# Order of the first batches' loads, v products and transposes, and place of the output transposes, in an attention and MLP kernel on one core

## The chip, the core and the metric

The kernel runs on one core of a Trainium2 chip. A core has five engines that run their own instruction streams in order and wait for one another through semaphores: TensorE (PE in the profile, its weight loads PEld), VectorE (DVE), ScalarE (ACT), GpSimd (POOL) and SyncE (SP, which only issues DMAs here). The metric is the device time of one execution in microseconds; the time before is the median of five runs.

## The reference

Two stages in a row, in float32, with 8 batches, 8 heads, 576 positions and head size 64:

```python
scores = scale * np.matmul(q, k.transpose(0, 1, 3, 2))
log_f = np.log(np.clip(f, 0.0001, 1.0))
cum = np.cumsum(log_f, axis=-1)
decay = cum[:, :, :, None] - cum[:, :, None, :]
causal = np.triu(np.ones((S, S), dtype=bool), k=1)
scores = np.where(causal, -1000000000.0, scores + decay)
attn = softmax(scores)            # exp(scores - max), divided by its row sum
x = (attn @ v) with heads side by side: 4608 tokens x 512
h = x @ w_in                      # 512 x 2048
g = h * (1.0 / (1.0 + np.exp(-h)))
out = g @ w_out                   # 2048 x 512
```

## The kernel before

The decay between two positions splits into a factor of the row, which the softmax's division cancels, and a factor of the column, exp(-cum + half), which is multiplied into v. So v with an extra column of ones times these weights gives numerator and denominator of the softmax in one product, and no maximum is taken.

**Heads of the sequences.** The first 128 positions of each batch are handled first ("0" in the names: `turn0`, `scores0`, `out0`, `back0`), for all heads of a batch at once. `turn0(b, 0)` turns q and `turn0(b, 1)` turns k with 16 matmuls each; ScalarE copies the q part to `qT`, VectorE the k part to `kT`. `scores0` makes the scores (a mask is added before by `ban0` or multiplied later by `mask0`) and ScalarE takes the exponential. `convert_v0` multiplies v by the weights `w_bf` (GpSimd). `out0` multiplies the exponentials with that v, and VectorE divides. `back0` turns the result with TensorE, and a copy puts it into the input `x` of the MLP. Batches 0 to 3 are done ahead of all else; 4 to 7 in the two calls of `two_more`, between MLP pieces.

**Rest of the sequences.** The loop over `m` takes two steps `n` = 2m and 2m + 1, each a batch's pair of heads (`b, p = divmod(n, 4)`) with the positions from 128 on. `prepare(n)` issues, for pair n + 2, the casts to bf16 on GpSimd (`cast_qk`) and a DMA transpose on SP (`transposes`, tile `qkT`, three buffers), the loads of pair n + 4, and for the next batch the loads of v on SP and the v products `convert_v` on GpSimd. `scores(n, c)` does one of three parts of the scores and exponentials; `attend(n)` the products with v, and VectorE divides into `xr`. `back(m)` turns a pair's outputs into `x`: by seven TensorE transposes into the tile `tx` and two VectorE copies where `BY_DMA[m]` is false (m = 0 to 3 and 15), by two DMA transposes on SP otherwise.

**MLP.** The tokens are cut into 13 groups `g`: three of heads, one of each batch's rest, two of tails. For each group, M1 has 16 chunks (`m1_chunk`: four matmuls into `hp`, tanh on ScalarE into `th`, `(th + 1) * hp` on VectorE into `gt`), and M2 has four parts for each 128 tokens (`m2_part`: four matmuls of 512 columns into `po`; after the fourth part ScalarE copies `po` to `osb`, and a store is queued). One M1 chunk or one M2 part is a piece. The queued stores are issued on GpSimd's queue by `slot`.

**Order.** It is written out by hand: each engine runs its instructions in the order in which the program emits them. Pieces of the MLP are put between the attention's steps by `fill(us, least, ends)`: `plan` lists as many pieces as the estimated time `us` holds, `wanted` chooses between M1 and M2, and `ends = (1, 0)` asks for an M2 piece first. A group's M1 may start once the group is in `ready`. In the loop over m, `slot(us, 1, 0)` calls `fill`, then issues the stores that were queued before it, then counts down `pending`, the list of groups that become ready some slots after their `back`. All PSUM tiles of `hp`, `po`, `dn`, `tx`, `tp` share four buffers (tag "big"); `sc` has two of its own.

The weights of the MLP are loaded in quarters, converted to bf16 on the way, by DMAs on GpSimd's queue (`load_w_in(0)` to `(3)`, `load_w_out`); so are the heads' q and k and v of batches 2 to 7.

Of the kernel before, what the change touches and what calls it, by code (L numbers as in the profile page):

```python
# [18 lines left out]
def kernel(  # L19
# [10 lines left out]
    nc = tc.nc  # L30

    B, H, S, D = q.shape
# [5 lines left out]
    SM = 512  # L38
    ST = S - SM
# [148 lines left out]
    def load_w_in(i):  # L188
        c0, c1 = i * DFF // WQ, (i + 1) * DFF // WQ
        nc.gpsimd.dma_start(out=w_in_bf[:, :, c0:c1], in_=w_in_v[:, :, c0:c1])  # L190
# [29 lines left out]
    for i in range(2):  # L220
        for g in range(2):
            nc.vector.tensor_copy(
                out=sel[:, i, :].rearrange("p (u w r) -> p u w r", u=2, w=2)[:, g, :, :],
                in_=ident_bf[:, :].rearrange("p (r u i w) -> p u i w r", u=2, i=2, w=2)[
                    :, g, i, :, :
                ],
            )

    def keep_warm(n):
# [7 lines left out]
        out=f_sb[:, :], in0=f_sb[:, :], scalar1=1e-4, scalar2=1.0, op0=ALU.max, op1=ALU.min  # L237
# [3 lines left out]
    wexp = setup.tile([BH, S + ST], FP32, name="wexp")  # L241
    nc.scalar.activation(out=f_sb[:, :], in_=f_sb[:, :], func=ACT.Ln)

    def weights_scan():
        nc.vector.tensor_tensor_scan(
            out=cum[:, :],
            data0=f_sb[:, :],
            data1=f_sb[:, :],
            initial=0.0,
            op0=ALU.add,  # L250
            op1=ALU.bypass,
        )
        nc.vector.tensor_scalar_mul(out=half[:, :], in0=cum[:, S - 1 : S], scalar1=0.5)
        nc.scalar.activation(
            out=wexp[:, 0:S], in_=cum[:, :], func=ACT.Exp, bias=half[:, 0:1], scale=-1.0
        )
        nc.vector.tensor_scalar(
            out=ban[:, :, :],
            in0=tri[:, None, :].to_broadcast([P, NP, P]),
            scalar1=-1.0,  # L260
            scalar2=30000.0,
            op0=ALU.add,
            op1=ALU.mult,
        )
        nc.vector.tensor_copy(out=wexp[:, S : S + ST], in_=wexp[:, SM:S])

    def weights():
        wps = pbig.tile([P, NM + 1, BH], FP32, name="wps", tag="big")
# [9 lines left out]
    def turn0(b, i):  # L278
        src = qk0[b]
        if i == 0:  # L280
            qT0[b] = qktp.tile([P, NP, P], BF16, name="qT0", tag="qT0", bufs=2)
        dst, evac = ((qT0[b], nc.scalar.copy), (kT0[b], nc.vector.tensor_copy))[i]
        tp = pbig.tile([P, NP, NRUN, RUN], FP32, name="tp", tag="big")
        for c in range(RUN):
            for j in range(2):
                nc.tensor.matmul(  # L286
                    tp[j * D : (j + 1) * D, :, :, c].rearrange("p a r -> p (a r)"),
                    lhsT=src[:, i, c * D : (c + 1) * D],
                    rhs=sel[:, j, :],
                    start=True,  # L290
                    stop=True,
                )
        evac(
            out=dst[:, :, :].rearrange("p a t -> p (a t)"),
            in_=tp[:, :, :, :].rearrange("p a r c -> p (a r c)"),
        )

    def ban0(b):
        sc = psc.tile([P, 2, NP, P], FP32, name="sc", tag="sc")
        for i in range(2):  # L300
            nc.tensor.matmul(
                sc[:, i, :, :].rearrange("p a t -> p (a t)"),
                lhsT=ident_bf[:, :],
                rhs=ban[:, :, :].rearrange("p a t -> p (a t)"),
                start=True,
                stop=False,
            )
        return sc

    def scores0(b, sc=None):  # L310
        t = qT0.pop(b)
        fresh = sc is None
        u = upool.tile([P, 2, NP, P], BF16, name="u", tag="u")
        u0[b] = u
        if fresh:
            sc = psc.tile([P, 2, NP, P], FP32, name="sc", tag="sc")
        for p in range(NP):
            for i in range(2):
                r = slice(i * D, (i + 1) * D)
                nc.tensor.matmul(  # L320
                    sc[:, i, p, :],
                    lhsT=kT0[b][r, p, :],
                    rhs=t[r, p, :],
                    start=fresh,
                    stop=fresh or p == NP - 1,
                )
        nc.scalar.activation(
            out=u[:, :, :, :].rearrange("p i a t -> p (i a t)"),
            in_=sc[:, :, :, :].rearrange("p i a t -> p (i a t)"),
            func=ACT.Exp,  # L330
            scale=scale,
        )
# [4 lines left out]
            out=x, in0=x, in1=tri[:, None, :].to_broadcast([P, H, P]), op=ALU.mult  # L337
        )

    def convert_v0(b):  # L340
        nc.gpsimd.tensor_tensor(
            out=v0[b][:, :, :],
            in0=vf0.pop(b)[:, :, :],
            in1=w_bf[:, 0, b * H : (b + 1) * H, None].to_broadcast([P, H, D + 1]),
            op=ALU.mult,
        )
# [338 lines left out]
    def plan(us_):  # L685

        a, c, kinds = at["m1"], at["m2"], []
        while us_ > 0:
            k = wanted(a, c)
            if not k:  # L690
                break
            kinds.append(k)
            if k == 1 and M1[a][1] == 0:
                begin[M1[a][0]] = (0, c)
            us_ -= (4 * (GW[M1[a][0]] / 2.4 + 2.5) if k == 1 else 4 * (DM / 2.4 + 2.5)) / 1000
            a, c = a + (k == 1), c + (k == 2)
        return kinds

    def fill(us_, least=0, ends=(0, 0)):

        left = us_ + at["left"]
        kinds = plan(left)
        n2 = kinds.count(2)
        kinds += [0] * (least - len(kinds))
        if any(ends) and n2 and 0 not in kinds:
            e0 = 1 if ends[0] else 0
            e1 = 1 if ends[1] and n2 > e0 else 0
            n1, mid = len(kinds) - n2, []
            inner = n2 - e0 - e1
            for x in range(n1 + inner):  # L710
                mid.append(2 if (x + 1) * inner // (n1 + inner) > x * inner // (n1 + inner) else 1)
            if inner and mid[-1] == 2 and e1:
                mid = mid[::-1] if not (e0 and mid[0] == 2) else mid
            kinds = [2] * e0 + mid + [2] * e1
        for k in kinds:
            t = step(k)
            if t is None:
                at["left"] = 0.0
                return
            left -= t / 1000  # L720
        at["left"] = left
# [5 lines left out]
    turn0(0, 0)  # L727
    keep_warm(1)
    turn0(0, 1)
    bans = [ban0(0), ban0(1)]  # L730
    scores0(0, bans[0])
    weights()
    setup_pool.__exit__(None, None, None)
    gpool = ctx.enter_context(tc.tile_pool(name="gpool", bufs=2))
    convert_v0(0)
    load_w_in(0)
    turn0(1, 0)
    turn0(1, 1)
    turn0(2, 0)
    turn0(2, 1)  # L740
    scores0(1, bans[1])
    convert_v0(1)
    out0(0, apart=True)
    scores0(2, ban0(2))
    convert_v0(2)
    load_w_in(1)
    turn0(3, 0)
    turn0(3, 1)
    bans = ban0(3)
    out0(1, apart=True)  # L750
    scores0(3, bans)
    convert_v0(3)
    load_qk0(4)
    load_qk0(5)
    load_w_in(2)
# [46 lines left out]
    def two_more(b, banned):  # L802
        for x in range(2):
            turn0(b + x, 0)
            turn0(b + x, 1)
            fill(0.6, 1)
        for x in range(2):
            if banned:
                scores0(b + x, ban0(b + x))
            else:  # L810
                scores0(b + x)
                mask0(b + x)
            fill(0.6 if x == 0 else 2.0, 1 if x == 0 else 2)
        out0(b)
        fill(0.6, 1)
        out0(b + 1)
        fill(0.8, 2)
        back0(b, on_act)
        fill(0.6, 1)
        back0(b + 1, on_act)  # L820
        fill(0.6, 1)

    fill(5.0)
    two_more(4, True)
    ready.add(1)
    fill(5.0)
# [2 lines left out]
    fill(6.0)  # L829
    two_more(6, False)  # L830
    ready.add(2)
    fill(4.0)

# [22 lines left out]
    def slot(us_, *ends):  # L858
        n = len(stores)
        fill(us_, 0, ends)  # L860
        store(n)
        for x in pending:
            x[0] -= 1
        while pending and pending[0][0] == 0:
            ready.update(pending.pop(0)[1])

    for m in range(NQ):
        n = 2 * m
        piece = 1.7 if m < 2 else 2.4
        scores(n, 0)  # L870
        scores(n, 1)
        prepare(n)
        slot(piece, 1, 0)
        if m > 0:
            back(m - 1)
            if m % 2 == 0:
                b = m // 2 - 1
                pending.append([1 + BY_DMA[m - 1], [REST_OF[b]] + ([TAILS_OF[b][0]] if b == NM - 1 else [])])
        scores(n, 2)
        scores(n + 1, 0)  # L880
        prepare(n + 1)
        slot(piece, 1, 0)
        scores(n + 1, 1)
        scores(n + 1, 2)
        slot(piece, 1, 0)
        attend(n)
        attend(n + 1)
        slot(min(3.5, max(0.8, behind() - LAG)) if m > 1 else 0.8)
# [38 lines left out]
```

## Time and profile before

| what | value |
|---|---|
| five runs | 345.1, 345.39, 347.62, 348.03, 349.75 us |
| median | 347.62 us |
| the profiled execution | 347.92 us |
| its span, first to last instruction | 346.1 us |
| TensorE's mean granted clock | 0.995 of full speed |
| DMA over the span | 50.44 MB in 141,497 packets |

The page lists each engine's busy time and its share of the span, then for groups of instructions the line, the engine, the operation, what it writes and reads, the count, the busy time and the mean duration. The costliest groups:

```profile
L576 ACT ACTIVATE th<-hp 128x384 bf16<-128x384 f32 (+2 forms) x208 | 95.2, 478 | 85.7 <-PE hp L568 83.2
L577 DVE SCALAR_TENSOR_TENSOR gt<-th,hp 128x384 bf16<-128x384 bf16 (+2 forms) x208 | 105.0, 521 | 83.4 <-ACT th L576 80.4
L613 PE MATMUL po<-w_out_bf,gt 128*128 128x512 bf16 (+1 forms) x592 | 145.1, 374 | 0.0
L568 PE MATMUL hp<-x,w_in_bf 128*128 128x384 bf16 (+2 forms) x704 | 129.4, 324 | 0.2
```

The last figures of a line are the idle time of the engine just ahead of these instructions and what ended most of it. TensorE's two MLP lines wait for next to nothing; ScalarE's and VectorE's MLP lines wait for TensorE and for each other. TensorE's matmuls are pipelined, so a matmul's mean duration is longer than the distance between two of them.

### The profile page before, as it was taken

To read this page: it belongs to the slowest core of one execution; us is meant where nothing else is said; L and a number is where in the kernel's file an instruction comes from. 1 tells how busy PE (TensorE), PEld (TensorE's weight loads), DVE (VectorE), ACT (ScalarE), POOL (GpSimd) and SP (SyncE) were. 2 spreads that over 40 slices of the span, in tenths; PEclk is the share of its full clock that TensorE was granted. 3 is DMA by queue.
4 is the path that set the end of the run, shared out by engine and by line. 5 is a ranking of instruction groups with operands and counts; after the bars stand their busy time and mean duration, and the time that the engine had idled before them with its cause. 6 is when DMAs were issued, how large, how long until landed. Compare 5 with 4: busy or idle time off the path is not lost.

```text
span 346.1 us, 8892 instructions
## 1 busy us (share of the span) xinstructions
PE 336.8 (97%) x3567; PEld 199.6 (58%) x3567; DVE 182.0 (53%) x389; ACT 216.9 (63%) x401; POOL 128.5 (37%) x227
## 2 busy tenths in 40 slices
PE   8899999999999999999999999999999999999995
PEld 3645655577655566456555666656656565555654
DVE  4645835357457467545636644555655464344330
ACT  5746736777666857759749686585775934454431
POOL 8895316733618245227218108208320000001011
PEclk9989999999999999999999999999999999999999
DMA  8999998999789888889689889989822010001012
GB/s 153 197 184 216 166 200 118 217 252 177 168 176 204 188 185 177 172 185 182 156 190 190 161 163 218 162 183 213 160 69 65 11 62 31 32 31 63 30 53 71
DMA packets 141497, 50.44 MB, mean 146 GB/s; under 512 B 132368, under 2 KB 138768, under 8 KB 141456
## 3 DMA queue, kind: packets, MB, share of 16 engines
q1 hardware_dynamic: 131440, 32.70, 52.5%
q0 software_dynamic: 9856, 17.04, 21.3%
q8 instruction: 28, 0.46, 0.6%
q10 hardware_dynamic: 160, 0.13, 0.1%
q14 instruction: 13, 0.11, 0.1%
HBM read 36.85 MB, written 9.44 MB: 134 GB/s over the span
## 4 chain that ended last, share of the span: by engine, by line
PE 85%; DMA 6%; ACT 3%; DVE 2%; SPq 1%; issue 1%; POOL 1%; POOLq 0%; ACTq 0%
PE po L613 36%; PE hp L568 33%; PE sc L460 7%; PE dn L507 5%; DMA vf<-in_v_dram 3%; PE dn L516 3%; DMA qkb<-in_k_dram 1%; ACT u L464 1%; PE tp L286 1%; DMA qkT<-qkb 1%; DVE gt L577 1%; ACT th L576 1%; SPq L158 1%; DVE xq L375 1%; DVE ut L483 0%
## 5 line engine op out<-in xcount | busy, mean ns | idle before, releaser
L576 ACT ACTIVATE th<-hp 128x384 bf16<-128x384 f32 (+2 forms) x208 | 95.2, 478 | 85.7 <-PE hp L568 83.2
L577 DVE SCALAR_TENSOR_TENSOR gt<-th,hp 128x384 bf16<-128x384 bf16 (+2 forms) x208 | 105.0, 521 | 83.4 <-ACT th L576 80.4
L613 PE MATMUL po<-w_out_bf,gt 128*128 128x512 bf16 (+1 forms) x592 | 145.1, 374 | 0.0
L568 PE MATMUL hp<-x,w_in_bf 128*128 128x384 bf16 (+2 forms) x704 | 129.4, 324 | 0.2
L568 PEld LDWEIGHTS <-w_in_bf 128*128 128x128 bf16 x832 | 80.2, 98 | 56.8 <-issue 3.1
L464 ACT ACTIVATE u<-sc 128x1024 bf16<-128x1024 f32 (+1 forms) x96 | 75.1, 821 | 12.7 <-PE sc L460 12.7
L613 PEld LDWEIGHTS <-gt 128*128 128x128 bf16 x592 | 53.4, 98 | 49.0 <-issue 3.0
L592 POOL DMA_DIRECT2D out_dram<-osb x38 | 21.0, 553 | 134.2 <-ACT osb L623 100.3
L414 POOL TENSOR_TENSOR vp<-vf,w_bf 128x520 bf16<-128x520 f32 (+1 forms) x32 | 34.6, 1082 | 27.7 <-DMA vf<-in_v_dram 19.5
L469 DVE TENSOR_TENSOR u<-u,tri 128x768 bf16<-128x768 bf16 x32 | 22.3, 697 | 21.8 <-ACT u L464 21.7
L623 ACT ACTIVATE osb<-po 128x512 f32<-128x512 f32 (+1 forms) x37 | 22.0, 595 | 17.2 <-PE po L613 17.2
L400 POOL CAST qkb<-qf 128x384 bf16<-128x384 f32 x32 | 17.0, 530 | 36.6 <-DMA qf<-in_q_dram 35.8
L460 PE MATMUL sc<-qkT 64*128 64x128 bf16 (+1 forms) x640 | 26.8, 207 | 0.2
L483 DVE TENSOR_TENSOR ut<-ut,trit 128x128 bf16<-128x128 bf16 x32 | 9.7, 304 | 31.4 <-ACT ut L476 30.9
L460 PEld LDWEIGHTS <-qkT 64*128 64x128 bf16 x640 | 18.3, 94 | 11.3 <-issue 8.9
L476 ACT ACTIVATE ut<-sc 128x640 bf16<-128x640 f32 x32 | 23.3, 727 | 0.0
L507 PEld LDWEIGHTS <-u 128*128 128x128 bf16 x576 | 20.7, 97 | 3.7 <-issue 1.1
L507 PE MATMUL dn<-vp,u 128*128 128x65 bf16 x384 | 21.8, 193 | 0.0
L507 PE MATMUL dn<-v,u 128*128 128x65 bf16 x192 | 19.8, 193 | 0.8 <-DVE gt L577 0.8
L525 DVE TENSOR_TENSOR xr<-dn,rec 128x448 bf16<-128x448 f32 x32 | 20.0, 625 | 1.1
L400 POOL CAST qkb<-kf 128x384 bf16<-128x384 f32 x32 | 17.4, 543 | 5.3 <-DMA kf<-in_k_dram 5.0
L568 PE MATMUL hp<-xt,w_in_bf 128*128 128x256 bf16 x128 | 17.7, 273 | 0.0
(68 smaller groups left out, 203.3 us busy)
## 6 DMA issues: line engine op xcount, KB each, us to landing
out_dram<-osb POOLq DMA_DIRECT2D x32, 256.0 KB, 2.9
vf<-in_v_dram SPq DMA_DIRECT2D x26, 256.0 KB, 5.3
qf<-in_q_dram SPq DMA_DIRECT2D x64, 96.0 KB, 2.8
kf<-in_k_dram SPq DMA_DIRECT2D x64, 96.0 KB, 3.0
w_in_bf<-in_moe_w_in_dram POOLq DMA_DIRECT2D x4, 512.0 KB, 7.0
w_out_bf<-in_moe_w_out_dram POOLq DMA_DIRECT2D x4, 512.0 KB, 9.3
vf<-in_v_dram POOLq DMA_DIRECT2D x6, 256.0 KB, 10.1
qkb<-in_q_dram POOLq DMA_DIRECT2D x8, 128.0 KB, 4.8
```

The lines of the kernel that those rows point to most:

```text
L400: nc.gpsimd.tensor_copy(out=t2[:, c0 : c0 + NR, :].rearrange("p c x -> p (c x)"), in_=t[:, :, :, :].rearrange("p c h d -> p (c h d)"),)
L414: nc.gpsimd.tensor_tensor(out=vbf[b][r, c, :, :], in0=vst[b][c][r, :, :], in1=w_bf[r, c + 1, b * H : (b + 1) * H, None].to_broadcast([n, H ...
L460: nc.tensor.matmul(sc[:, i, o : o + q1 - q0], lhsT=kt, rhs=t[r, q0:q1], start=True, stop=True)
L464: nc.scalar.activation(out=u[:, :, c * SM : c * SM + w], in_=sc[:, :, 0:w], func=ACT.Exp, scale=scale)
L469: nc.vector.tensor_tensor(out=x, in0=x, in1=tri[:, None, None, :].to_broadcast([P, 2, NR, P]), op=ALU.mult,)
L476: nc.scalar.activation(out=ut[:, :, 0:3:2, :].rearrange("p k i t -> p i k t"), in_=sc[:, :, T0 : T0 + (NM + 1) * ST].rearrange("p i (k t) ...
L507: nc.tensor.matmul(dn[:, i * NR + c - 1, :], lhsT=u[:, i, o : o + P], rhs=vals(kb, i), start=(kb == 0), stop=(kb == c),)
L568: nc.tensor.matmul(hp[:, :], lhsT=w_in_bf[:, cc, fc * P : (fc + 1) * P], rhs=xcols(g, cc), start=(cc == 0), stop=(cc == NCC - 1),)
L576: nc.scalar.activation(out=th[:, :], in_=hp[:, :], func=ACT.Tanh, scale=0.5)
L577: nc.vector.scalar_tensor_tensor(out=gt[:, fc, :], in0=th[:, :], scalar=1.0, in1=hp[:, :], op0=ALU.add, op1=ALU.mult,)
L613: nc.tensor.matmul(po[:, :], lhsT=gt[:, fc, tb * P : (tb + 1) * P], rhs=w_out_bf[:, fc, m0:m1], start=(fc == 0), stop=(fc == NFC - 1),)
L623: nc.scalar.activation(out=osb[:, :], in_=po[:, :], func=ACT.Copy, scale=0.5)
```

## The change

In the setup: the copy of the tail weights into `wexp` comes after the turning of batch 0. The first quarter of `w_in` is issued on GpSimd's queue ahead of all v products, the second ahead of those of batches 2 and 3. The v product of batch 0 runs on VectorE, behind the cast of `kT` of batch 1; those of batches 1, 2 and 3 on GpSimd follow. Batch 3's q is turned ahead of batch 0's outputs, its k behind the scores of batch 2.

In `fill`: where `ends` is given, a plan without an M2 piece has its first piece replaced by one (`step` takes it if one is to be had), and the rest of the plan is spread around it as before.

In the loop over m: of the first slot one piece, an M2 part if there is one, comes ahead of `back(m - 1)` and the rest behind it; since that rest counts as the slot, a group enters `ready` one slot earlier. In `two_more(6, False)` a fill is 2.8 instead of 2.0, and the last fill ahead of the loop 3.2 instead of 4.0.

The counts of matmuls, tanh, products and DMAs are the same; all five engines do the same work, but for the one v product, in another order. On GpSimd four stores instead of three come ahead of the casts for n = 3.

```diff
-        nc.vector.tensor_copy(out=wexp[:, S : S + ST], in_=wexp[:, SM:S])
...
-    def convert_v0(b):
-        nc.gpsimd.tensor_tensor(
+    def convert_v0(b, engine=nc.gpsimd):
+        engine.tensor_tensor(
...
         kinds = plan(left)
-        n2 = kinds.count(2)
         kinds += [0] * (least - len(kinds))
-        if any(ends) and n2 and 0 not in kinds:
+        if any(ends) and kinds:
+            if 2 not in kinds:
+                kinds[0] = 2
+            n1, n2 = len(kinds) - kinds.count(2), kinds.count(2)
             e0 = 1 if ends[0] else 0
             e1 = 1 if ends[1] and n2 > e0 else 0
-            n1, mid = len(kinds) - n2, []
             inner = n2 - e0 - e1
-            for x in range(n1 + inner):
-                mid.append(2 if (x + 1) * inner // (n1 + inner) > x * inner // (n1 + inner) else 1)
-            if inner and mid[-1] == 2 and e1:
-                mid = mid[::-1] if not (e0 and mid[0] == 2) else mid
+            n = n1 + inner
+            mid = [2 if (x + 1) * inner // n > x * inner // n else 1 for x in range(n)]
+            if inner and mid[-1] == 2 and e1 and not e0:
+                mid = mid[::-1]
             kinds = [2] * e0 + mid + [2] * e1
...
     turn0(0, 1)
+    nc.vector.tensor_copy(out=wexp[:, S : S + ST], in_=wexp[:, SM:S])
     bans = [ban0(0), ban0(1)]
     scores0(0, bans[0])
     weights()
     setup_pool.__exit__(None, None, None)
     gpool = ctx.enter_context(tc.tile_pool(name="gpool", bufs=2))
-    convert_v0(0)
     load_w_in(0)
     turn0(1, 0)
     turn0(1, 1)
+    convert_v0(0, nc.vector)
+    convert_v0(1)
+    load_w_in(1)
     turn0(2, 0)
     turn0(2, 1)
     scores0(1, bans[1])
-    convert_v0(1)
+    turn0(3, 0)
     out0(0, apart=True)
     scores0(2, ban0(2))
+    turn0(3, 1)
     convert_v0(2)
-    load_w_in(1)
-    turn0(3, 0)
-    turn0(3, 1)
+    convert_v0(3)
     bans = ban0(3)
     out0(1, apart=True)
     scores0(3, bans)
-    convert_v0(3)
...
-            fill(0.6 if x == 0 else 2.0, 1 if x == 0 else 2)
+            fill(0.6 if x == 0 else 2.0 if banned else 2.8, 1 if x == 0 else 2)
...
-    fill(4.0)
+    fill(3.2)
...
-        slot(piece, 1, 0)
+        fill(0.2, 1, (1, 0))
         if m > 0:
             back(m - 1)
             if m % 2 == 0:
                 b = m // 2 - 1
                 pending.append([1 + BY_DMA[m - 1], [REST_OF[b]] + ([TAILS_OF[b][0]] if b == NM - 1 else [])])
+        slot(piece - 0.2)
```

## The prediction

> **What bounds the kernel now.** I read the page's engine totals and its chain of waits, cut the span into stretches to see where TensorE is not busy, and read those places in the timeline.
>
> ```profile
> PE 336.8 (97%) x3567; PEld 199.6 (58%) x3567; DVE 182.0 (53%) x389; ACT 216.9 (63%) x401; POOL 128.5 (37%) x227
> ...
> PE 85%; DMA 6%; ACT 3%; DVE 2%; SPq 1%; issue 1%; POOL 1%; POOLq 0%; ACTq 0%
> ```
>
> TensorE is busy 97% of the span and carries 85% of the chain. The change adds and removes no matmul, so it can only win or lose TensorE's gaps, 9.3 us in all (346.1 - 336.8), and time at a lowered clock. The stretches (TensorE's busy time is the second number; the clock granted stands third from the end):
>
> ```profile
> 15.15:18.56 3.41, 1.94 (x24) 1.13 (x21) 2.23 (x7) 2.44 (x5) 3.32 (x6) 1.00 1.13 178
> 18.56:21.98 3.42, 3.42 (x10) 1.23 (x9) 0.69 (x1) 0.96 (x2) 3.37 (x6) 0.50 1.27 175
> ...
> 84.00:88.00 4.00, 3.57 (x45) 2.44 (x44) 3.05 (x6) 3.15 (x8) 3.33 (x4) 1.00 1.23 186
> ...
> 100.00:112.00 12.00, 10.43 (x140) 6.61 (x138) 9.00 (x18) 8.23 (x16) 7.53 (x11) 1.00 1.10 196
> 112.00:140.00 28.00, 28.00 (x327) 16.33 (x327) 17.25 (x35) 19.56 (x35) 11.40 (x20) 1.00 0.87 181
> ```
>
> Three holes: 1.47 us at 15 to 18.6, followed by 3.4 us at half clock; 0.43 at 84 to 88; 1.57 at 100 to 112. From 112 to 280 there is none, so a new order has nothing to win there. The 3.7 us from 280 on lie behind the last M2 parts, whose order stays. The timeline names what ends the holes:
>
> ```profile
> 15.24 1.04 POOL L341 TENSOR_TENSOR v<-vf,w_bf 128x520 bf16<-128x520 f32 x1 [0.60 <-DMA vf<-in_v_dram]
> ...
> 16.34 0.42 PE L360 MATMUL dn<-v,u 128*128 128x65 bf16 x8 [0.69 <-POOL v L341]
> ...
> 18.26 7.03 PE L568 MATMUL hp<-x,w_in_bf 128*128 128x512 bf16 x24
> ```
>
> ```profile
> 99.28 2.12 PE L568 MATMUL hp<-x,w_in_bf 128*128 128x384 bf16 x12
> ...
> 101.53 1.48 DVE L577 SCALAR_TENSOR_TENSOR gt<-th,hp 128x384 bf16<-128x384 bf16 x3 [0.74 <-ACT th L576]
> 102.13 0.55 PE L549 MATMUL tx<-ident_bf,xr 128*128 128x128 bf16 x7 [0.73 <-DVE gt L577]
> ...
> 106.82 2.11 PE L568 MATMUL hp<-x,w_in_bf 128*128 128x384 bf16 x12
> ...
> 109.77 0.19 PE L507 MATMUL dn<-v,u 128*128 128x65 bf16 x1 [0.84 <-DVE gt L577]
> ```
>
> Both late holes have one pattern: three M1 chunks (12 matmuls) straight after scores. Their tanh waits behind the exponentials, gt behind that, and the next tile (tx, dn) waits until gt frees a PSUM buffer. The hole at 86.17 is the same: three chunks, then tx released by gt.
>
> [...] the 3.41 us stretch with TensorE busy for 1.94 is followed by exactly one stretch at 0.50, with 10 matmuls where the next has 24. [...] `ut<-ut,trit` took 0.23 us alone and 1.42 at 107.83, beside two 1.05 us v products on GpSimd. That prices the v product that moves to VectorE.
>
> **Part 1, first batches.** Nothing is removed; one v product changes engine.
> - Copy of the tail weights (0.33 us) behind the kT cast. It ends near 8.5 instead of 7.41; the weight transposes needed it at 8.51. Cost 0 to 0.1.
> - v product of batch 0 on VectorE, between the casts of batches 1 and 2. GpSimd took 1.05. [...] It starts at 10.8 and may wait for GpSimd's batch-1 product (now about 9.9 to 10.95). The cast of batch 2, 10.99 before, starts near 11.65: +0.65 on scores and exponential of batch 2. Turning half of batch 3 ahead of the first outputs wins part of it back: by the durations in the timeline batch 3's exponential ends near 15.9, was 15.66.
> - GpSimd's queue: w_in quarters 0 and 1 are issued about 1.6 and 2.9 us earlier (9.1, 11.0). DMA is loaded above its share of 1.0 in all these stretches, and both quarters stand behind v of batches 2 and 3, so their landing moves little. The batch-3 product no longer stands behind a 0.80 us issue, but it began at 15.24 because v landed at 15.10 (issue 8.17, chain: 6.93 us); if v lands alike it starts alike. Queue behind it: loads of batches 4 and 5, not on the path.
> - So the first M1 matmul at 18.26 moves by -0.4 (v lands earlier) to +0.65 (VectorE decides): I take 0, and the half-clock stretch stays, since TensorE's work between 12 and 18 us stays the same.
>
> **Part 2, M2 piece first, outputs turned behind it.**
> - Every slot of the attention loop opens with an M2 piece (0.86 us) that needs neither ScalarE nor VectorE at once. In the pair at 99.28 the order M1,M1,M1,tx becomes M2,tx,M1,M1, and at 106.82 M2 with two chunks takes the place of M2 with three. Both waits should go: -0.9 (end of the twelfth matmul's issue to tx) and -1.0. What is late next there: the keys and queries of the next pairs landed 3.8 to 4.4 us before their scores, so 1.9 us fit.
> - The wait at 86.17 (0.5) goes too, but the scores right behind it waited anyway: the transposed qkT, issued at 83.15, took 3.9 us and landed at 87.04, and scores started again at 87.09. Win 0 to 0.5; I take 0.
> - GpSimd's queue: four stores instead of three now stand ahead of the casts for the pair n = 3 (three took 1.69, casts from 68.67). One more is +0.55 on the casts; their qkT landed at 75.75 (69.89 + 5.9) just as scores wanted it. So TensorE pays 0 to 0.55; I take 0.3. SP's order of transposes and loads stays; later pairs have 3.8 us of slack.
> - An M1 group is released one slot earlier. The two groups fed by DMA transposes that move most are those of batches 2 and 3: first matmul 150.64, less two attentions (1.71) and an M2 part (0.86), is 148.0; its third matmul needs x at 148.4 and x landed at 148.45 (142.67 + 5.8). Batch 3: 178.65 less 3.4 is 175.2, x landed at 175.4 (171.91 + 3.5). Cost 0 to 1; I take 0, since transposes on TensorE's side leave at least 1 us for batches 0 and 1.
> - Fill sizes 2.8 and 3.2 instead of 2.0 and 4.0 move M2 pieces within a stretch in which TensorE was busy 23.88 of 24.00 us (60 to 84): 0; with that cover gone, no more than one piece, 0.9.
>
> **Sum**: -0.9 - 1.0 + 0.3 = -1.6. The profiled execution took 347.9 (span 346.1 and 1.8 around it), so 346.3; that run is 0.3 above the median 347.6, on which it is **346.0**. About 1%, 3.5 us, is what a measurement of this kernel can tell from no change.
>
> **The rivals.**
> - A, as summed, 0.42: 346.0. Its unknown costs span -2.4 (casts cost nothing, 86.17 wins) to about 0; with the head's -0.4 and +0.65 its own range is 343.9 to 348.0.
> - B, the head quickens, 0.30: the v of batch 3 lands early, its product no longer stands behind an issue, TensorE is busy enough at 15 to 18 us, and the half-clock stretch never comes: 3.4/2 = -1.7, M1 0.4 earlier, and the 0.3 isn't paid: 346.0 - 2.4 = 343.6, faster. For it: POOL's order puts products 2 and 3 together. Against: the landing at 15.10 is a DMA's, and the edits don't speed it.
> - C, nothing shown, 0.12: the holes only move, to x of batches 2 and 3 (-1.9 given back) and the casts: 347.5. The edit doing less than it says is here too.
> - D, slower, 0.16: GpSimd blocks at the fourth store. If its M2 output isn't ready, the casts for n = 3 wait, and all behind them (transposes, v loads, next casts) is late by as much; TensorE runs dry. Such waits reach 9.3 us elsewhere on this queue. It decides from about 5.4 us on (3.5 + 1.9 won elsewhere); at 6.3 us it gives 347.6 + 6.3 - 1.9 = 352.0. Against: in the trace this store followed at 69.81 without a wait.
>
> **How the numbers follow.** Faster by over 1% (below 344.1): B 0.30, and the low edge of A, 0.05: 0.35. Slower by over 1% (above 351.1): D, 0.16. Within: the rest of A and C, 0.49. The range 342.9 to 348.6 leaves out D and the outer edge of B, about 0.2.
>
> **What would show it.** Right: no TensorE wait on gt before tx or dn at 84 to 112, that stretch 1.5 to 2.4 us shorter; a scores wait on qkT near 76 and 87; the first M1 matmul within half a microsecond of 18.3; one half-clock stretch behind it. Wrong: the clock stays whole there (B); GpSimd idle before a store at 66 to 72 (D); matmuls of `hp` waiting for a DMA transpose near 148 or 175 (C).

## The result: slower by 0.4%, one long wait in place of three short ones

| | before | after |
|---|---|---|
| median | 346.53 us, 79 runs | 348.03 us, 44 runs |
| lowest to highest | 344.27 to 349.75 | 344.26 to 350.66 |
| after / before | | 1.004, 95% interval 1.0028 to 1.0053 |
| the profiled execution | 347.92 (span 346.1) | 345.62 (span 343.8) |

The five runs shown ahead of the prediction had a median of 347.62; 79 runs have 346.53. The profiled execution of after is one of its quickest, 2.4 us under its own median, so its page alone shows a gain, not the loss. The ratio on record leaves out executions that took over 1.5% longer than the fastest of the same kernel. The engine totals, the chain and two groups of the profiled execution:

```profile
PE 335.1 (97%) x3567; PEld 198.9 (58%) x3567; DVE 184.0 (54%) x390; ACT 217.4 (63%) x401; POOL 128.4 (37%) x226
...
PE 71%; DMA 14%; POOL 6%; SPq 5%; issue 2%; ACT 0%; DVE 0%; POOLq 0%
...
L567 PE MATMUL hp<-x,w_in_bf 128*128 128x384 bf16 (+2 forms) x704 | 128.7, 321 | 1.2 <-DMA x<-xr 0.6
...
L459 PE MATMUL sc<-qkT 64*128 64x128 bf16 (+1 forms) x640 | 26.7, 207 | 1.0 <-DMA qkT<-qkb 0.9
```

The chain now has 14% DMA (6% before): it runs through loads and transposes, where it ran along TensorE. The stretches that had the holes (busy times of PE, PEld, DVE, ACT, POOL with instruction counts, then clock, DMA share, GB/s):

```profile
84.00:88.00 4.00, 3.10 (x37) 1.88 (x36) 2.62 (x6) 3.13 (x6) 3.32 (x5) 1.00 0.84 148
100.00:112.00 12.00, 11.91 (x156) 7.33 (x155) 8.03 (x17) 8.88 (x17) 7.36 (x11) 1.00 0.89 188
112.00:140.00 28.00, 28.00 (x321) 16.22 (x320) 16.17 (x32) 19.41 (x36) 10.72 (x19) 1.00 0.99 193
15.15:18.56 3.41, 2.73 (x32) 1.44 (x29) 2.42 (x7) 2.63 (x5) 3.41 (x7) 1.00 1.24 207
18.56:21.98 3.42, 3.42 (x18) 1.53 (x17) 2.07 (x3) 2.27 (x4) 3.23 (x7) 1.00 1.22 190
```

The hole at 100 to 112 is closed (1.57 to 0.09 us), as predicted. The head is busier than before (2.73 against 1.94) and at full clock in this execution. The stretch at 84 to 88 got worse, and so did one place near 173. TensorE's timeline there (start, duration, then what ended the idle time before):

```profile
83.87 0.61 PE L567 MATMUL hp<-x,w_in_bf 128*128 128x256 bf16 x4 [0.38 <-DVE xt L554]
...
84.51 0.28 PE L459 MATMUL sc<-qkT 64*128 64x64 bf16 x8
85.69 0.40 PE L459 MATMUL sc<-qkT 64*128 64x128 bf16 x8 [0.90 <-DMA qkT<-qkb]
...
173.32 1.14 PE L567 MATMUL hp<-x,w_in_bf 128*128 128x384 bf16 x6 [0.61 <-DMA x<-xr]
```

What an ordinary execution of after looks like had to come from further runs. Each run also lists its mean granted TensorE clock. One whole stretch of 3.41 us at half clock lowers that mean by 3.41 x 0.5 / 346 = 0.005, so I count a mean under 0.9975 as at least one such stretch. A part of one at the end of the span lowers the mean too (to 0.998 in the profile of `three stores, more pieces`), so the few executions at 0.997 (3 of the 46 counted for after, 2 of the 27 for before) are uncertain. This **half-clock share** is given with each run below.

### The profile page after: what moved, and what is told of

It is laid out like the page before. It is cut to its first block, busy times and chain, and to the rows that moved or that the text cites. A ratio compares the mean times of both kernels' runs of the same rounds, so it can differ in the third digit from the quotient of the medians.

```text
span 343.8 us, 8894 instructions
## 1 busy us (share of the span) xinstructions
PE 335.1 (97%) x3567; PEld 198.9 (58%) x3567; DVE 184.0 (54%) x390; ACT 217.4 (63%) x401; POOL 128.4 (37%) x226
## 4 chain that ended last, share of the span: by engine, by line
PE 71%; DMA 14%; POOL 6%; SPq 5%; issue 2%; ACT 0%; DVE 0%; POOLq 0%
PE po L612 31%; PE hp L567 28%; PE sc L459 6%; DMA vf<-in_v_dram 4%; PE dn L506 4%; DMA w_out_bf<-in_moe_w_out_dram 3%; DMA qktf<-in_k_dram 3%; SPq L158 3%; PE dn L515 2%; DMA kf<-in_k_dram 2%; POOL qkb L131 2%; DMA x<-xr 2%; DMA qkT<-qkb 1%; SPq L168 1%; SPq L427 1%
## 5 line engine op out<-in xcount | busy, mean ns | idle before, releaser
L468 DVE TENSOR_TENSOR u<-u,tri 128x768 bf16<-128x768 bf16 x32 | 21.6, 676 | 22.3 <-ACT u L463 22.3
L482 DVE TENSOR_TENSOR ut<-ut,trit 128x128 bf16<-128x128 bf16 x32 | 11.7, 366 | 29.8 <-ACT ut L475 29.8
```

Source lines behind the costliest of these rows:

```text
L468: nc.vector.tensor_tensor(out=x, in0=x, in1=tri[:, None, None, :].to_broadcast([P, 2, NR, P]), op=ALU.mult,)
```

## Experiments

All times are medians in us; each ratio is to the kernel before, run beside it on the same chip: 346.74 (half-clock share 13 of 67) beside changed kernel again, the two halves and dummy work in the head; 346.61 (9 of 67) beside the third set and the last three of the table; 346.53 (5 of 58) beside the other four. Kernels beside different ones are best compared by their ratios. A ratio need not be the quotient of the two medians: for dummy work in the head these are level, and the ratio is 1.0021.

| kernel | runs | median | ratio and interval | half-clock share |
|---|---|---|---|---|
| changed kernel again | 14 | 347.32 | 1.0013 (0.9989 to 1.0037) | 6 of 14 |
| changed kernel, third set | 22 | 347.32 | 1.0021 (1.0003 to 1.0039) | 11 of 22 |
| head alone | 22 | 347.26 | 1.0006 (0.9987 to 1.0025) | 1 of 22 |
| fills and loop alone | 22 | 347.95 | 1.0032 (1.0010 to 1.0053) | 13 of 22 |
| after, dummy work in the head | 22 | 346.75 | 1.0021 (1.0002 to 1.0040) | 6 of 22 |
| after, three stores ahead of the casts | 22 | 346.15 | 0.9994 (0.9973 to 1.0014) | 6 of 22 |
| M2 put first, alone | 22 | 345.43 | 0.9967 (0.9949 to 0.9986) | 2 of 22 |
| three stores, more pieces | 13 | 344.91 | 0.9956 (0.9939 to 0.9972) | 1 of 13 |
| after, dummy work in the wait at n = 3 | 14 | 346.53 | 1.0005 (0.9982 to 1.0027) | 1 of 14 |
| after, outputs turned ahead as before | 22 | 346.09 | 0.9989 (0.9971 to 1.0006) | 4 of 22 |
| three stores, groups ready later | 22 | 346.70 | 1.0002 (0.9982 to 1.0023) | 9 of 22 |
| outputs turned ahead, more pieces | 15 | 346.26 | 0.9989 (0.9969 to 1.0009) | 1 of 15 |

### The changed kernel again

No edit.

> The whole change again, on the chip on which its parts run. Both theories: about 1.0 to 1.8 us slower than the kernel before in the median (346.5 and 348.0 so far); a mean clock near 0.995, one half-clock stretch, in some 6 of 10 executions.

> The changed kernel as it is, beside the other three on one chip. Ratio 1.001 to 1.005 and a half-clock stretch in 0.4 to 0.7 of the executions if the loss belongs to the kernel; under 1.0 and a share under 0.3 if it belonged to the chips on which it was run before.

Both repeats are above before, by less than in the first set and than was expected; the interval of the third set leaves out no change, that of the first repeat doesn't. Over all three sets 46 of 80 executions had a half-clock stretch (first set 29 of 44), against 27 of 192 of the kernel before beside these experiments. The profiled execution of the first repeat, 348.01 us, is an ordinary one. Its group lines for the scores and for the tiles whose waits were to go (count, busy time and mean, idle before):

```profile
L459 PE MATMUL sc<-qkT 64*128 64x128 bf16 (+1 forms) x640 | 26.8, 207 | 2.8 <-DMA qkT<-qkb 2.7
...
L506 PE MATMUL dn<-v,u 128*128 128x65 bf16 x192 | 19.8, 193 | 0.1
...
L548 PE MATMUL tx<-ident_bf,xr 128*128 128x128 bf16 x35 | 2.8, 219 | 0.0
```

In the profile of before the same three groups read:

```profile
L460 PE MATMUL sc<-qkT 64*128 64x128 bf16 (+1 forms) x640 | 26.8, 207 | 0.2
...
L507 PE MATMUL dn<-v,u 128*128 128x65 bf16 x192 | 19.8, 193 | 0.8 <-DVE gt L577 0.8
...
L549 PE MATMUL tx<-ident_bf,xr 128*128 128x128 bf16 x35 | 2.8, 219 | 1.1 <-DVE gt L577 1.1
```

So 1.8 us of waits ahead of dn and tx went, and 2.6 us more of waiting ahead of the scores came. The new one is a single wait, ahead of the scores of pair n = 3, in TensorE's timeline of the repeat:

```profile
73.38 0.28 PE L459 MATMUL sc<-qkT 64*128 64x64 bf16 x8
76.35 0.40 PE L459 MATMUL sc<-qkT 64*128 64x128 bf16 x8 [2.69 <-DMA qkT<-qkb]
76.68 1.63 PE L612 MATMUL po<-w_out_bf,gt 128*128 128x512 bf16 x4
```

An M2 part behind the wait takes 1.63 instead of 1.04 us. The stretches around it show why:

```profile
73.56:76.98 3.42, 0.73 (x18) 0.41 (x11) 0.98 (x3) 1.43 (x5) 1.23 (x3) 1.00 0.78 139
76.98:80.39 3.41, 3.41 (x18) 1.68 (x18) 0.98 (x2) 1.55 (x3) 1.40 (x3) 0.50 0.90 210
```

TensorE is busy for 0.73 of 3.42 us, and the next 3.41 us run at half clock: half of them, 1.7 us, is lost on top of the wait. What TensorE waits for comes through GpSimd's queue; its timeline in the same execution:

```profile
64.70 2.53 POOL L413 TENSOR_TENSOR vp<-vf,w_bf 128x520 bf16<-128x520 f32 x2 [0.63 <-DMA vf<-in_v_dram]
67.17 2.22 POOL L591 DMA_DIRECT2D out_dram<-osb  x4
69.44 0.50 POOL L399 CAST qkb<-qf 128x384 bf16<-128x384 f32 x1
```

Read downwards it is a chain: v lands, the last two v products run, four stores are issued, the casts follow, SP issues the DMA transposes at 70.66, and they land at 76.30. In the quick profile of after the same three steps stand at:

```profile
62.10 2.38 POOL L413 TENSOR_TENSOR vp<-vf,w_bf 128x520 bf16<-128x520 f32 x2 [0.18 <-DMA vf<-in_v_dram]
64.43 2.23 POOL L591 DMA_DIRECT2D out_dram<-osb  x4
66.71 0.50 POOL L399 CAST qkb<-qf 128x384 bf16<-128x384 f32 x1
```

There v landed 2.6 us sooner, qkT at 73.25, and TensorE didn't wait at n = 3 at all. So where v lands late, this lane and not TensorE sets when n = 3 can start, and the landing varies by microseconds from execution to execution. One execution each (the first store is where the v products end):

| execution | first store | stores ahead | casts | qkT lands | TensorE waits at n = 3 |
|---|---|---|---|---|---|
| before | 66.94 | 3 | 68.67 | 75.75 | 0.2 |
| after, quick | 64.43 | 4 | 66.71 | 73.25 | none |
| after, repeat | 67.17 | 4 | 69.44 | 76.30 | 2.7 |
| after, third set | 67.09 | 4 | 69.36 | 76.46 | 2.3 |
| three stores | 66.38 | 3 | 68.11 | 75.20 | 1.5 |
| M2 first alone | 65.67 | 3 | 67.40 | 74.37 | 0.5 |
| outputs turned ahead | 66.94 | 3 | 68.67 | 76.21 | 2.2 |

In the profile of before TensorE was itself late, by the half-clock stretch in its head (1.7 us), and met qkT as it landed. That was the view on which the prediction was built, and only 27 of 192 executions of before have such a stretch, in the head or elsewhere. There is no profile of before without one; M2 first alone, whose order on TensorE is meant to be that of before up to 85 us, waits 0.5 us at n = 3.

### The two halves of the change

`head alone` is before with the new setup and first batches, without the new `fill`, fill sizes and loop:

```diff
-    convert_v0(0)
     load_w_in(0)
...
+    convert_v0(0, nc.vector)
+    convert_v0(1)
+    load_w_in(1)
...
+    turn0(3, 0)
     out0(0, apart=True)
     scores0(2, ban0(2))
+    turn0(3, 1)
```

> Part 1 alone (order of the first batches' loads, products and turns), with the loop as before. Theory H (the head costs it: the half-clock stretch behind the head comes in more executions): 1 to 1.7 us slower than before, and a clock of 0.995 in more executions than the kernel before. Theory L (the loop costs it: scores wait for qkT and M1 for x, because they come earlier in TensorE's order): 0 to 0.5 us faster than before.

`fills and loop alone` is the opposite, with the head of before:

```diff
-        if any(ends) and n2 and 0 not in kinds:
+        if any(ends) and kinds:
+            if 2 not in kinds:
+                kinds[0] = 2
...
-        slot(piece, 1, 0)
+        fill(0.2, 1, (1, 0))
         if m > 0:
             back(m - 1)
...
+        slot(piece - 0.2)
```

> Part 2 alone (M2 piece first in every slot, outputs turned behind one piece, groups released a slot earlier, fill sizes), with the head as before. Theory H: no slower than before, down to 1.9 us faster as predicted. Theory L: 1.5 to 2.5 us slower than before, and the profile shows TensorE idle before scores by qkT near 76 to 87 us and before hp by x near 148 to 175 us, more than the 1.9 us that it wins at 101 and 109.

The loop has the loss alone: 1.0032, and 13 of 22 executions with a half-clock stretch. In its profile the waits for gt ahead of tx and dn are gone and scores wait 2.5 us for qkT, as theory L had it; the waits for x that it had besides are not there (0.4 us ahead of all `hp` matmuls).

The ratio of the head can't be told from no change. That doesn't show the head to be free: its 21 executions without a half-clock stretch have a median of 347.2, the 54 such executions of before beside it one of 346.5, which its few stretches (1 of 22) partly hide. In its profile the waits for gt at 101.83 and 109.47 are still there (0.73 and 0.84 us, as in before), and it waits another 0.9 us for v products on GpSimd at 53 to 55, behind a fill that is still 2.0; none of the other profiles, those of after with 2.8 among them, has this wait. Whether it is what the head costs was not tried.

### Which edit in the loop

`M2 put first, alone` is before with the new `fill` and nothing else.

> The kernel before with the new fill alone (an M2 piece first in each slot even where the plan had none); the outputs are turned where they were, groups ready when they were, fill sizes and first batches as before. TensorE's order differs from before only from pass 2 on, so nothing ahead of 85 us changes. The predicted gain by itself: the wait ahead of tx near 101 us (0.9) goes; the one ahead of the products near 109 (1.0) may stay, since three M1 chunks still come ahead of tx one slot later. Theories S and G: 0 to 1.0 us faster than before, and a half-clock stretch as often as before (2 of 10). If it is slower than before by 1 us, the forced M2 pieces themselves cost and both theories fall.

Faster than before by 0.3%, with 2 of 22 half-clock stretches. The gain that the prediction summed is there, though it measures 1.1 us (346.53 to 345.43) where the sum had 1.9: in its profile the waits for gt at 101 and 109 are gone (dn waits 0.0, tx 0.3 in all).

`after, outputs turned ahead as before` undoes only the place of `back(m - 1)`; the fourth store and the earlier readiness go with it:

```diff
-        fill(0.2, 1, (1, 0))
+        slot(piece, 1, 0)
         if m > 0:
             back(m - 1)
...
-        slot(piece - 0.2)
```

> Changed kernel, but the outputs of a pair are turned ahead of the whole first slot again, as before: the fourth store ahead of the casts for n = 3 and the earlier readiness go with it; the new head, the M2 piece put first and the two fills stay. Lane theory (the casts and the DMA transpose set scores(n=3), a long wait there halves the clock, the fourth store makes it long): ratio 0.996 to 0.999, half-clock stretch in under 0.25 of the executions, wait for qkT of n=3 0.8 to 1.8. If the new head is what costs (TensorE arrives too early, whatever the store): ratio 1.001 or more and a share over 0.4.

Beside the changed kernel on one chip: 346.09 against 347.32, and 4 of 22 half-clock stretches against 11 of 22. So turning the outputs behind the first piece, with what goes with it, brings the loss. The profiled execution still waits 2.2 us for qkT at n = 3, longer than expected, with three stores ahead; so the fourth store isn't the whole of the wait.

`after, three stores ahead of the casts` keeps TensorE's order of after and leaves the store of the new first piece to the next slot:

```diff
-    def slot(us_, *ends):
-        n = len(stores)
+    def slot(us_, *ends, queued=None):
+        n = len(stores) if queued is None else queued
...
+        queued = len(stores)
         fill(0.2, 1, (1, 0))
...
-        slot(piece - 0.2)
+        slot(piece - 0.2, queued=queued)
```

> The whole change, but the stores issued by the first slot of each pass are those that were queued before its first M2 piece: three stores, not four, ahead of the casts for n = 3 on GpSimd; TensorE's order is untouched. Theory S (the fourth store makes qkT for n = 3 late, and that decides): the wait of scores for qkT near 74 us shrinks by about 0.55 us or more, the half-clock stretch comes in 2 of 10 executions or fewer, and the time is 1 us or more below the whole change, near before. Theory G (that qkT lands when the DMA lane gets to it; TensorE merely reaches it some 2 us earlier, and the one long wait halves the clock): the landing moves by 0.5 us or less, the half-clock stretch comes in 4 of 10 or more, and the time is within 0.6 us of the whole change.

0.9994: level with before. Its interval overlaps those of the two repeats, not that of the first set (from 1.0028). The wait is 1.5 us in its profile, and 6 of 22 executions have a half-clock stretch, between what the two theories had, so this run doesn't decide between them. `three stores, groups ready later` besides makes a group ready one slot later, as before (`1 + BY_DMA[m - 1]` becomes `2 + BY_DMA[m - 1]`):

> Three stores ahead of the casts for n = 3, as in the run with one store fewer, and besides a group's M1 becomes ready one slot later, as before the change. If the earlier readiness costs what is left (x of batch 3 waited for near 173, 0.8 to 1.1): that wait is under 0.3 and the time is 0.5 to 1.0 under the run with three stores alone (346.15), ratio 0.996 to 0.998. If the wait only moves to another place: no difference to that run, ratio 0.998 to 1.001.

The wait for x near 173, 0.9 us in the profile with three stores, is gone, and the ratio is no lower: 1.0002 against 0.9994. It isn't a loss that shows.

### Is it the clock?

`after, dummy work in the head` adds four dummy matmuls to the gaps of the first batches (`keep_warm(1)` behind `back0` of batches 1 and 2, `keep_warm(2)` behind that of batch 3).

> The whole change plus four matmuls of 512 columns on zeros in the gaps of TensorE between the outputs of batches 1 to 3 and the first M1 matmul (0.9 us of work in 1.3 us of gaps; the output doesn't change). Theory H: no half-clock stretch (clock 0.999 to 1.0 in nearly all executions), 1.0 to 1.7 us faster than the whole change, so equal to before or better. Theory L: the clock stays whole too, but the time is still over that of before by 0.5 us or more, since the loop's waits stay.

6 of 22 half-clock stretches, where both theories had nearly none, and a ratio of 1.0021: inconclusive. `after, dummy work in the wait at n = 3`:

```diff
         scores(n, 2)
+        if m == 1:
+            keep_warm(8)
         scores(n + 1, 0)
```

> The whole change with eight matmuls on zeros (1.7 us at full clock) just ahead of the scores for n = 3, where TensorE waits for qkT anyway; they change no output. Both theories: the half-clock stretch follows from that one long wait, so it comes in 2 of 10 executions or fewer, and the median falls by about the half-clock loss times its share (1.7 x 0.4 = 0.7 us or more) below the whole change. If the stretch stays as often, the long wait isn't its cause.

Eight dummy matmuls, work that helps nothing, put ahead of the scores of n = 3: 1 of 14 half-clock stretches and a ratio of 1.0005. So most half-clock stretches of after do come from this wait. How much of the time comes back with them isn't shown: the interval, up to 1.0027, holds the ratios of both repeats.

Not every such wait is followed by half clock. In the repeat the clock fell at 76.98 and again behind the last matmul, at 346.63: 269.65 us, 79 times 3.413. In the profile of before it fell at 18.56 and at 346.24: 327.68 us, 96 times 3.413. Cut into windows of that length, each counted back from its own last fall of the clock, three executions read:

```profile
72.13:75.54 3.41, 1.49 (x26) 1.08 (x23) 2.01 (x6) 2.62 (x6) 1.46 (x3) 1.00 1.21 158
75.54:78.95 3.41, 3.24 (x17) 1.65 (x18) 0.56 (x1) 1.02 (x1) 1.61 (x3) 0.50 1.11 208
```

(three stores, groups ready later: a 2.1 us wait, all but 0.2 of it in one window, and half clock in the next)

```profile
72.65:76.06 3.41, 1.60 (x28) 1.20 (x25) 2.12 (x6) 2.73 (x6) 0.40 (x1) 1.00 1.29 129
76.06:79.47 3.41, 2.96 (x38) 1.88 (x39) 1.25 (x3) 2.09 (x4) 2.23 (x6) 1.00 1.13 222
```

(after, third set: 2.3 us, some 0.45 of it in the next window; the clock stays whole)

```profile
71.62:75.03 3.41, 2.41 (x31) 1.71 (x29) 1.73 (x5) 3.41 (x7) 1.09 (x2) 1.00 1.22 188
75.03:78.44 3.41, 2.18 (x22) 1.33 (x22) 1.06 (x4) 1.50 (x3) 1.27 (x4) 1.00 1.29 231
```

(outputs turned ahead: 2.2 us, cut in two by the window's edge; whole)

Of two waits of like length one costs 1.7 us more than the other. In these three a window with 1.49 us busy of 3.41 was followed by half clock, and windows with 1.60 and 2.41 were not; in the heads of before and of `outputs turned ahead, more pieces` windows with 1.94 and 2.18, of smaller matmuls, were followed by it. So busy time alone doesn't tell which wait is followed by half clock, and what does wasn't shown.

### Real work in the wait

`three stores, more pieces` gives the slot behind `back` 2.0 us of pieces more at m = 1 and 1.0 at m = 2:

```diff
-        slot(piece - 0.2, queued=queued)
+        slot(piece - 0.2 + {1: 2.0, 2: 1.0}.get(m, 0.0), queued=queued)
```

> As the kernel with three stores, and 2.0 us more of MLP pieces ahead of the scores for n = 3 and 1.0 us more ahead of those for n = 5; the pieces come from later slots. Theory G: TensorE reaches both scores later by that much without loss, the waits for qkT near 74 and 86 us fall to under 0.5 us each, the half-clock stretch is gone (1 of 10 or fewer), and the time falls by 2 us or more below the whole change, to 345.0 or less, faster than before. Theory S: no further gain on the kernel with three stores.

0.9956, with 0.1 us of waiting for qkT in its profile: the fastest version here, faster than before by 0.3 to 0.6%, and 2.4 us under the repeats of the changed kernel, which ran on other chips. `outputs turned ahead, more pieces` adds 1.7 us to each slot of m = 1:

```diff
-        slot(piece, 1, 0)
+        slot(piece + (1.7 if m == 1 else 0.0), 1, 0)
```

> Outputs turned ahead of the whole first slot, as in the run with late stores, and 1.7 us of pieces more in each slot of m = 1. Lane theory: the pieces fill the waits for qkT of n=3 and n=5, each under 0.8; half-clock share under 0.15; ratio 0.994 to 0.997. If the waits for qkT are not what counts: ratio as in the run with late stores, or over it.

Waits for qkT and half-clock share fall as expected (0.1 us; 1 of 15), but the time doesn't: 0.9989, as without the pieces. Its profiled execution doesn't tell why: it is the one of the 15 with a half-clock stretch (18.66 to 22.07, behind the head), and it has 0.5 us each of other waits, for gt ahead of dn and for the v product in the head. What takes the gain was not tried.

## Why the prediction was wrong

The prediction had a change of -1.6 us and 346.0; measured are +1.5 (348.03 - 346.53) and 348.0. Its steps:

- **Waits for gt, -0.9 and -1.0: right that they go, but too large.** They go, here and where M2 is put first alone, which gains 1.1 us of the 1.9.
- **Holes only move, to x: it happens, and isn't the cause.** The wait for x of batch 3 near 173 came (0.6 us in one of the three profiles of after, 0.9 with three stores), as case C had it. Later readiness won nothing.
- **Head, 0: open.** Alone it gives 1.0006, but at full clock it is 0.7 us slower than before. The first M1 matmul came at 17.86 to 17.90 in three executions of after, within the half microsecond given. The half-clock stretch in the head, which was to stay, is in none of the three profiles of after; it had been read from an execution with such a stretch, which only one in seven has. That was the sign of rival B, whose gain didn't come.
- **v product on VectorE: the wait was named, its size not.** The cast of batch 2 near 11.65, and with it the +0.65, was the author's estimate; no trace had shown the product on VectorE. It took 0.69 to 1.58 us in the eleven profiles that have it. In the quick profile of after it took 0.89 us and ended 0.57 us after the GpSimd product beside it (11.55 against 10.98), and the cast of batch 2 started at 11.47, 0.48 us later than in before (10.99). The `ut` operation of 1.42 us that the prediction puts beside two v products ran beside the first alone and ended 0.09 us after it (109.25 against 109.16); the one at 104.04 took 0.85 us and ended 0.08 us after the v product beside it (104.89 against 104.81). These fit a VectorE operation that waits the GpSimd product out, as the prediction allowed; no run tried it by itself.
- **Wait at 86.17, win 0 to 0.5, taken 0.** Waits for qkT of n = 5 were 0.9 and 0.7 us in two of the three profiles of after: a loss was left out.
- **The failed step: "GpSimd's queue ... So TensorE pays 0 to 0.55; I take 0.3."** It priced the fourth store by what the casts lose, on the ground that qkT "landed at 75.75 ... just as scores wanted it". Two things were wrong in it. The coincidence belonged to an execution in which TensorE was 1.7 us late; in seven others TensorE stops at n = 3 at 73.6 to 74.3 while qkT lands at 74.4 to 76.5. There it has no slack: a later cast is paid in full, and whatever TensorE wins ahead of this place comes back as waiting. (In the quick profile of after qkT came in time, and in that of dummy work in the head TensorE waited only 0.3 us.) And the price of a wait was taken as its length. The sum put the gains of 101 and 109 beside a short wait at 76; in fact the lane held TensorE for 2.3 to 2.7 us in two of three profiled executions, and in the repeat such a wait cost another 1.7 us of clock, a term that the sum doesn't have at all.
- **The range of case A** doesn't follow from its terms: -2.4 and -0.4 from 347.6 give 344.8, not 343.9, so A had no part below 344.1.

How the loss divides: over the 80 executions, those of after with a half-clock stretch had a median of 348.2 and those without 346.9; of before, 347.8 and 346.5. A stretch costs about 1.3 us, and (46/80 - 27/192) x 1.3 = 0.6 us is the share of the clock. About 0.4 (346.9 - 346.5) is left in executions at full clock; that the longer waits eat the gain there is read from the profiles, not shown by a run. The means differ by 1.0 (347.7 and 346.7). Rival D had the place right, GpSimd's stores ahead of the casts of n = 3, and the mechanism wrong: the stores never blocked (four in 2.22 us), and the loss was 1.5 us where it gave 4.4 (352.0 - 347.6).

A half-clock stretch in mid-kernel lasted 3.41 us (76.98 to 80.39 in the repeat) and costs up to half of that, 1.7 of 346 us, or 0.5%. But 1.7 us is more than the prediction's whole sum.

What stays open: how much of the loss is the fourth store and how much the shorter way to `back` on TensorE, since the intervals of these kernels overlap; whether it is the head, slower at full clock, that leaves the kernel with outputs turned ahead at 0.9989 where M2 first alone has 0.9967 (overlapping too), or the fills of 2.8 and 3.2, which were not tried alone; and what sets the landing of v, on which the lane starts.

## What to carry to other kernels

An engine that is 97% busy can still be paced at a few places by another lane: before adding up the waits that a new order removes, look, in more than one execution, at where the next transfer from outside lands, for gains ahead of it are only lent. Merging short waits into one long one wasn't neutral on TensorE (in the repeat 1.8 us of them went, and one of 2.7 us and 1.7 us of lost clock came): here the best time came from putting other work into that wait (0.9956), though a second try with other amounts gained nothing (0.9989). A profile taken in an unusual execution (a half-clock stretch that one in seven has) shows slack and coincidences that the others don't have.

## What had not been expected of the hardware

- One wait of 2.1 to 2.7 us in a stream that is otherwise full was followed by 3.41 us at half clock in some executions (waits of 2.7 and 2.1 us) and not in others (2.3 and 2.2 us): after had a half-clock stretch somewhere in 58% of its executions, before in 14%.
- The same v loads landed 2.6 us apart in two executions of one kernel (the last v products began at 62.10 and 64.70), and the DMA transpose for n = 3 took from 5.2 us from issue to landing (fills and loop alone) to 6.3 (outputs turned ahead, 69.89 to 76.21); in the quick profile of after it took 5.3 (67.93 to 73.25).
